# Attention and expert kernel on one core: k transposed by the DMA crossbar, one store transfer per tile, a sixth load buffer, new engine orders

## The chip, the cores and the metric

One core of a Trainium2 chip. The metric is the device time of one execution in microseconds, the median of several. Every experiment was timed in rounds beside runs of the kernel before on the same chip. A ratio is the mean time of one kernel's fast runs over the mean time of the other's fast runs in the same rounds, so it is not quite the ratio of the medians quoted beside it. The interval behind a ratio is the 95% interval. Medians are over all runs of a kernel, slow ones included.

In the profile, PE is TensorE (matrix products and transposes), PEld its weight loads, DVE is VectorE, ACT ScalarE, POOL GpSimd and SP SyncE. A `q` behind an engine's name is its instruction queue. PSUM is where the program puts the tiles that TensorE writes. The granted clock is the share of its full clock that the profile records for TensorE. A transpose by the DMA crossbar is what the traces record as DMA_TRANSPOSE.

## The reference, cut to what matters

```python
def _attn_ref(q, k, v):                      # 8 batches, 8 heads, 576 positions, 64 wide
    scores = (1 / sqrt(64)) * q @ k^T
    ret = scores * Dmat                      # Dmat = gamma[h] ** (i - j) for i >= j, else 0
    return ret @ v

def _moe_ref(x, w_in, w_out, g_ln):          # 4608 tokens, 512 -> 1024 -> 512
    h = x @ w_in
    e = exp(h - max(h)); solu = h * e / (sum(e) + 1e-9)
    ln = (solu - mean) / sqrt(var + 1e-6) * g_ln
    return ln @ w_out                        # float32 [4608, 512], 9.4 MB
```

The first result, with the heads side by side in the columns, is the x of the second part.

Of the kernel before, what the change touches and what calls it, by code (L numbers as in the profile page):

```python
# [10 lines left out]
F16 = mybir.dt.float16  # L11
P = 128
# [1 line left out]

DUR = dict(
    T=0.45, L=0.45, M1=1.73, M2=1.73, I=0.23, S=0.23, V=0.23, K=0.14, G=0.1,
    qe=1.0, xe=0.59, ex=1.22, le=1.0, oe=0.69, wi=0.6, wg=0.66, cva=0.6,
    mask=1.22, st_a=0.29, so=1.22, bn=1.68, od=0.7, wib=0.55, wgd=0.5, WM=1.73, nw=0.62, wf=0.66, wp=1.04, sqd=0.7, gc=0.2,
    sq=1.03, sk=1.03, st_b=0.4, cast=0.84, rs=0.6, cv=0.61,
    ld=0.89, ldw=1.34, out=0.72, lm=0.42,  # L20
)
PE_OUT = 0.2
PER = 5.36
START = dict(SP=2.3)
WARM = 31.0
NE = 14

FIRST = dict(
    ACT=(
        "cv0 qe0 cv1 qe1 xe0 wi1a wi2a wi0a xe1 wi3a ex0 qe2 wg0 le0 wg2 qe3 wg4 wg6 ex1 xe2 "  # L30
        "nw1 nw0 xe3 qe4 wf1 ex2 qe5 wf3 le1 xe4 qe6 wf2 ex3 le2 xe5 oe0 qe7 wf0 ex4 le3 xe6 "
        "qe8 ex5 le4 xe7 qe9 oe1 ex6 le5 oe2 qe10 xe8 ex7 le6 xe9 qe11 oe3 ex8 le7 oe4 wf6 "
        "qe12 xe10 wf4 ex9 le8 xe11 oe5 wf7 qe13 ex10 le9 xe12 wf5 qe14 oe6 ex11 le10 xe13 "
        "oe7 qe15 oe8 ex12 le11 xe14 qe16 oe9 ex13 le12 xe15 qe17 oe10 ex14 le13"
    ),
    DVE=(
        "gc sq0 sa0 sd0 sq1 mask0 wi1b sa1 sd1 mask1 wi2b wi0b wi3b sa2 sd2 so0 mask2 wg1 sa3 "
        "sd3 wg3 wg5 wg7 mask3 so1 bn0 sa4 sd4 bn1 mask4 so2 od0 sa5 sd5 mask5 bn2 sa6 sd6 "
        "so3 mask6 od1 bn3 sa7 sd7 so4 mask7 od2 bn4 sa8 sd8 so5 mask8 bn5 sa9 sd9 so6 od3 "
        "mask9 bn6 so7 od4 sa10 sd10 mask10 bn7 so8 od5 sa11 sd11 mask11 bn8 sa12 so9 sd12 "  # L40
        "od6 mask12 bn9 sa13 sd13 so10 od7 mask13 bn10 so11 sa14 sd14 od8 bn11 mask14 so12 "
        "sa15 sd15 od9 mask15 bn12 so13 od10 mask16 bn13 so14"
    ),
    PE=(
        "G K0 T0 S0 T1 I0 V0 K1 S1 I1 V1 M1_0 T2 K2 S2 L0 I2 V2 K3 T3 M1_1 S3 WM I3 V3 K4 T4 "
        "M1_2 S4 T5 M2_0 L1 I4 V4 K5 S5 T6 M1_3 I5 V5 K6 S6 L2 M2_1 T7 M1_4 I6 V6 K7 S7 L3 "
        "M2_2 T8 M1_5 I7 V7 K8 S8 L4 M2_3 T9 M1_6 I8 V8 K9 L5 S9 T10 M1_7 L6 I9 M2_4 V9 K10 "
        "S10 T11 M1_8 L7 I10 M2_5 V10 K11 S11 T12 M1_9 L8 I11 V11 K12 S12 M2_6 T13 M1_10 I12 "
        "V12 K13 S13 L9 M2_7 T14 M1_11 I13 L10 M2_8 V13 K14 S14 T15 M1_12 L11 M2_9 I14 V14 "
        "K15 S15 T16 M1_13 L12 I15 S16 V15 M2_10 T17 M1_14 L13 I16 S17 V16 M2_11"  # L50
    ),
    POOL=(
        "sk0 sk1 sm0 sc0 sm1 sc1 sq2 sk2 cv2 sk3 sm2 sc2 cv3 sq3 sm3 sc3 sk4 sq4 cv4 sq5 sk5 "
        "sm4 sc4 sq6 rs0 cv5 sk6 sq7 sm5 sc5 cv6 cv7 sk7 sm6 sk9 sc6 sk8 sq8 wp0 rs1 sm7 sc7 "
        "cv8 sq9 cv10 cv9 wp3 sm8 sk10 sc8 cv12 wp2 sq10 sq11 sq12 sm9 sc9 sk11 cv11 sk12 wp1 "
        "sm10 sc10 sk13 rs2 sq13 sq14 cv14 sm11 sc11 sk14 rs3 wp6 sm12 sc12 cv13 sq16 cv15 "
        "cv16 sm13 sc13 wp4 sk15 sq15 sk16 wp5 rs4 sm14 sc14 sq17 wp7 sk17 rs5 cv17 sm15 sc15 "
        "sq18 sk18 cv18 sq19 sk19 cv19"
    ),
    SP=(  # L60
        "ldk0 ldv0 ldq0 ldk1 ldq1 lm ldv1 lwi1 lwi2 lwi0 lwi3 ldq2 ldk2 ldv2 ldk3 lwo0 ldv3 "
        "ldq3 lwo2 lwo4 lwo6 ldk4 ldq4 ldv4 ldq5 ldk5 ldq6 ldv5 ldk6 ldv7 ldq7 ldq9 ldk7 ldk8 "
        "ldv6 ldq10 ldv8 ldk9 ldq11 ldq8 ldv10 ldk10 ldv11 ldq14 ldk11 ldk14 ldv9 ldv12 ldq12 "
        "ldk12 ldk13 ldq16 out0 out1 ldk17 ldv16 ldq15 ldq13 ldv13 out2 ldv14 ldq17 ldk16 "
        "out4 ldv15 ldk15 out3 out5 out7 out6 ldv17 ldv18 ldq19 ldk18 ldv19 ldq18 ldk19 ldq20 "
        "out8 ldk20 ldv20 out9 ldq21 ldk21 ldv21"
    ),
)
HOP = 0.06
# [104 lines left out]
def kernel(  # L174
# [10 lines left out]
    nc = tc.nc  # L185
    B, H, S, D = q.shape
    NTOK, DM = out.shape
    DFF = moe_w_in.shape[1]
    ACT = mybir.ActivationFunctionType
# [2 lines left out]
    small_np, masks_np, id_np = _np_tables()  # L192


    CAP = dict(raw=5, qk16=3, v16=4, tp=1, qkT=3, s=1, ret=2, xy=1, gw=6, s160=4, s161=9, tt=2,
               xT=5, h=1, e=2, oc=2, solu=3, sml=8, lnT=4, o=1, osb=3)
    pools = {}
    PS = bass.MemoryType.PSUM
# [13 lines left out]
    NT = 2 * NW  # L212
# [22 lines left out]
    st = [dict() for _ in range(NS)]  # L235
    tk = [dict() for _ in range(NT)]
# [43 lines left out]
    def cast_v(i, copy):  # L280
        t = pools["v16"].tile([P, 4, 2, D], F16, tag="v16", name="v16")
        copy(out=t, in_=st[i]["vr"])
        st[i]["v16"] = t

    def qk_tp(i):
        d = st[i]
        tp = pools["tp"].tile([P, 2, 2, 2, P], F16, tag="tp", name="tqk")
        for n, src in enumerate((d["q16"], d["k16"])):
            for hp in range(2):
                for j in range(2):  # L290
                    nc.tensor.transpose(  # L291
                        out=tp[:, n, hp, j], in_=src[:, j, 2 * hp : 2 * hp + 2, :], identity=ident
                    )
        d["tp"] = tp

    def qk_ev(i):
        d = st[i]
        d["qkT"] = pools["qkT"].tile([P, 2, 2, 2, P], F16, tag="qkT", name="qkT")
        nc.scalar.copy(out=d["qkT"], in_=d["tp"])  # L299


    ee = [slice(0, 64), slice(64, 128)]
# [34 lines left out]
    def scores(i):  # L337
        d = st[i]
        s_ps = pools["s"].tile([P, 2, 2, 2, P], FP, tag="s", name="s_ps")
        sv = s_ps.rearrange("p e h j (a q) -> p e h j a q", a=2)  # L340
        qkT = d["qkT"]
        for hp in range(2):
            for j in range(2):
                for c in range(2):
                    for e in range(2):
                        nc.tensor.matmul(  # L346
                            out=sv[ee[c], e, hp, j], lhsT=qkT[ee[e], 1, hp, j, ee[c]],
                            rhs=qkT[ee[e], 0, hp, :, ee[c]], start=True, stop=True,
                        )
        d["s"] = s_ps  # L350
# [171 lines left out]
    def store(t):  # L522
        w, c = divmod(t, 2)
        b, wi = wins[w]
        for j in range(2):
            q_dma = nc.scalar if t == NT - 1 and j else nc.sync
            if wi < 2:
                r0 = b * S + 256 * wi + P * c
                q_dma.dma_start(
                    out=out[r0 : r0 + P, :].rearrange("(q j) m -> j q m", j=2)[j],  # L530
                    in_=tk[t]["osb"][64 * j : 64 * j + 64],
                )
            else:
                for r in range(2):
                    r0 = (b + 2 * c + r) * S + 512
                    q_dma.dma_start(
                        out=out[r0 : r0 + 64, :].rearrange("(q j) m -> j q m", j=2)[j],
                        in_=tk[t]["osb"][64 * j + 32 * r : 64 * j + 32 * r + 32],
                    )
# [39 lines left out]
    def op(name, eng, kind, deps, key, emit, bufs=()):  # L579
        key = rank.get(name, PER * key[0] + key[1])  # L580
        ops.append(Op(name, eng, DUR[kind], [x for x in deps if x], key, emit, bufs))

    for i in range(NS):
        w, hf = divmod(i, 2)
        b, wi = wins[w]
        full = wi < 2
        op(f"ldq{i}", "SP", "ld", [], (i - 5, 0.0), lambda i=i: load(i, "q", q), [("rawq", [f"sq{i}"])])
        op(f"ldk{i}", "SP", "ld", [], (i - 5, 0.1), lambda i=i: load(i, "k", k), [("rawk", [f"sk{i}"])])
        op(f"ldv{i}", "SP", "ld", [], (i - 5, 0.2), lambda i=i: load(i, "v", v), [("rawv", [f"cv{i}"])])
        early = i < 2  # L590
        op(f"sq{i}", "DVE" if early else "POOL", "sqd" if early else "sq", [f"ldq{i}"], (i - 2, 1.8),
           lambda i=i, e=nc.vector if early else nc.gpsimd: scale(i, "q", 0, e), [("q16", [f"T{i}"])])
        op(f"sk{i}", "POOL", "sk", [f"ldk{i}"], (i - 2, 2.9), lambda i=i: scale(i, "k", 32, nc.gpsimd),
           [("k16", [f"T{i}", f"K{i}" if full else ""])])
        op(f"cv{i}", "ACT" if early else "POOL", "cva" if early else "cv", [f"ldv{i}"], (i - 1, 0.0),
           lambda i=i, c=nc.scalar.copy if early else nc.gpsimd.tensor_copy: cast_v(i, c),
           [("v16", [f"V{i}", f"K{i}" if full else ""])])
        op(f"T{i}", "PE", "T", [f"sq{i}", f"sk{i}"], (i - 1, 2.73), lambda i=i: qk_tp(i), [("tp", [f"qe{i}"])])
        op(f"qe{i}", "ACT", "qe", [f"T{i}"], (i - 1, 3.6), lambda i=i: qk_ev(i), [("qkT", [f"V{i}"])])
        op(f"S{i}", "PE", "S", [f"qe{i}"], (i, 0.3), lambda i=i: scores(i), [("s", [f"mask{i}"])])  # L600
        op(f"mask{i}", "DVE", "mask", [f"S{i}", "lm"], (i, 3.2), lambda i=i: mask(i), [("ret", [f"V{i}"])])
        if full:
            op(f"K{i}", "PE", "K", [f"sk{i}", f"cv{i}"] + [f"V{i - 1}" if i else ""], (i, 0.8), lambda i=i: kv_mm(i))
# [15 lines left out]
    for t in range(NT):  # L619
        w, c = divmod(t, 2)  # L620
        m = t + 2
# [18 lines left out]
    for c in range(4):  # L640
# [4 lines left out]
        out=masks, in_=nc.inline_tensor(masks_np, name="masks").ap().rearrange("p (m j) -> p m j", m=2)))  # L645
# [75 lines left out]
```

## The kernel before: what the change touches

The sequence is cut into 18 windows. Each has two halves of the heads, which gives 36 attention steps `i`, and two tiles of 128 tokens, which gives 36 expert tiles `t`. Sixteen windows are full, so 32 of the tiles are full. The other four tiles collect the short ends of several sequences.

Within a tile the tokens are stored even ones first: partition `64*j + q` holds row `2*q + j` of the output. This is why the store needs a pattern in `j`.

The instructions of each engine stand in an order that lists in the kernel fix (`FIRST`, cut here), with a small scheduler for the rest.

```python
def qk_tp(i):                                  # TensorE transposes q and k: eight of 128x128
    tp = pools["tp"].tile([P, 2, 2, 2, P], F16, tag="tp", name="tqk")
    for n, src in enumerate((d["q16"], d["k16"])):
        for hp in range(2):
            for j in range(2):
                nc.tensor.transpose(out=tp[:, n, hp, j],
                    in_=src[:, j, 2 * hp : 2 * hp + 2, :], identity=ident)

def qk_ev(i):                                  # ScalarE brings both out of PSUM
    nc.scalar.copy(out=d["qkT"], in_=d["tp"])

def x_ev(i):                                   # the attention result, tokens in (j, q) order
    nc.scalar.copy(out=d["xT"].rearrange("p c h q -> p c (h q)"), in_=d["av"][:, :, 0:256])

def store(t):                                  # two transfers of 64 rows for each tile
    for j in range(2):
        q_dma = nc.scalar if t == NT - 1 and j else nc.sync
        if wi < 2:
            q_dma.dma_start(
                out=out[r0 : r0 + P, :].rearrange("(q j) m -> j q m", j=2)[j],
                in_=tk[t]["osb"][64 * j : 64 * j + 64])
        else: ...                              # short tiles: four transfers of 32 rows
# ... loads: one transfer of 256 KB for each of q, k, v and full step, all issued by SyncE
```

The softmax here doesn't subtract the row's maximum and nothing guards it: scores larger than these inputs give would overflow.

## Time and profile before

| | before |
|---|---|
| median of 4 runs | 225.87 us (225.39 to 226.43) |
| span of the profiled run | 224.9 us |
| TensorE busy | 207.0 us (92%) |
| granted TensorE clock | 0.996 |
| a store, issue to landing | 2.4 us |

These lines are from the page of the kernel before. They give TensorE's and VectorE's busy time, then the busy tenths in 40 slices of 5.6 us (TensorE, granted clock, DMA), and the packets by size.

```profile
PE 207.0 (92%) x2985; PEld 121.8 (54%) x2985; DVE 181.5 (81%) x320; ACT 163.2 (73%) x238; POOL 151.8 (67%) x231
PE   7776989899699999699999999999999999999991
PEclk9999999999999999999999999999999999999998
DMA  6999999995576610799988776777763552222324
DMA packets 65635, 42.64 MB, mean 190 GB/s; under 512 B 4024, under 2 KB 59456, under 8 KB 65600
```

TensorE is nearly full from the eighteenth slice on and has no idle time at all from 106 to 205 us (busy 99.00 of 99 us). The DMA is full in the first quarter and once more, for three slices, around 105 us. Of the 4,024 packets under 512 B, 3,769 are of four bytes. The trace also records 3,761 increments of semaphores by DMA, so I take them for completion packets. In the queue q1 they are 3,696, sixteen for each of its 231 transfers. If every DMA engine that a transfer uses posts one, they count the engines of each transfer.

The next lines come from two queries of the same trace. The first is the TensorE timeline around 148 us (start, duration, line, out<-in). The second is the table of stretches (stretch, length, busy time of each engine, clock, DMA share, GB/s).

```profile
148.09 0.39 PE L291 MATMUL tqk<-ident,q_3298 128*128 128x128 f16 x4
148.31 0.39 PE L291 MATMUL tqk<-ident,k_3340 128*128 128x128 f16 x4
148.54 1.89 PE L431 MATMUL h_ps<-w_in_122,xT 128*128 128x512 f16 x8
...
153.91 1.89 PE L431 MATMUL h_ps<-w_in_122,xT 128*128 128x512 f16 x8
```

```profile
40.00:106.00 66.00, 61.20 (x952) 37.12 (x941) 62.40 (x102) 51.41 (x76) 57.72 (x82) 1.00 0.68 187
106.00:180.00 74.00, 74.00 (x1159) 45.58 (x1159) 63.53 (x114) 57.32 (x84) 56.41 (x89) 1.00 0.73 202
```

One tile follows the other at 5.37 us here. The eight transposes start at 148.09 and the next group of matmuls at 148.54, so they cost TensorE 0.45 us. Their pipelined durations overlap and must not be added up. Taking four of the eight away is worth 0.22 us a step, where TensorE alone decides. From 40 to 106 us VectorE is as full as TensorE (62.4 and 61.2 of 66 us).

The section of DMA issues of the same page shows KB for each transfer and the median time from issue to landing:

```profile
qr<-in_q_dram SPq DMA_DIRECT2D x32, 256.0 KB, 4.8
out_dram<-o_sb SPq DMA_DIRECT2D x64, 128.0 KB, 2.4
```

### The profile page before, as it was taken

To read this page: it belongs to the slowest core of one execution; us is meant where nothing else is said; L and a number is where in the kernel's file an instruction comes from. 1 tells how busy PE (TensorE), PEld (TensorE's weight loads), DVE (VectorE), ACT (ScalarE), POOL (GpSimd) and SP (SyncE) were. 2 spreads that over 40 slices of the span, in tenths; PEclk is the share of its full clock that TensorE was granted. 3 is DMA by queue.
4 is the path that set the end of the run, shared out by engine and by line. 5 is a ranking of instruction groups with operands and counts; after the bars stand their busy time and mean duration, and the time that the engine had idled before them with its cause. 6 is when DMAs were issued, how large, how long until landed. Compare 5 with 4: busy or idle time off the path is not lost.

```text
span 224.9 us, 7378 instructions
## 1 busy us (share of the span) xinstructions
PE 207.0 (92%) x2985; PEld 121.8 (54%) x2985; DVE 181.5 (81%) x320; ACT 163.2 (73%) x238; POOL 151.8 (67%) x231
## 2 busy tenths in 40 slices
PE   7776989899699999699999999999999999999991
PEld 2433445556455556465666666665666666555440
DVE  6654788999999998999999888888887888876540
ACT  3555889776869988578787777777777777776751
POOL 3429599899989989829578869695968677311010
PEclk9999999999999999999999999999999999999998
DMA  6999999995576610799988776777763552222324
GB/s 176 360 344 348 320 262 287 286 279 157 128 224 173 195 24 13 188 305 293 267 235 247 215 195 192 214 191 191 218 184 109 153 131 52 50 47 60 84 69 119
DMA packets 65635, 42.64 MB, mean 190 GB/s; under 512 B 4024, under 2 KB 59456, under 8 KB 65600
## 3 DMA queue, kind: packets, MB, share of 16 engines
q1 hardware_dynamic: 65200, 41.96, 66.9%
q8 instruction: 23, 0.38, 0.8%
q10 hardware_dynamic: 400, 0.21, 0.5%
q14 instruction: 12, 0.10, 0.2%
HBM read 32.71 MB, written 9.44 MB: 187 GB/s over the span
## 4 chain that ended last, share of the span: by engine, by line
PE 63%; DVE 17%; DMA 9%; POOL 4%; issue 2%; SPq 2%; ACT 1%; DVEq 0%; POOLq 0%; ACTq 0%
PE h_ps L431 21%; PE o_ps L501 21%; PE xy L311 6%; PE tln L480 5%; PE tqk L291 4%; DMA qr<-in_q_dram 4%; DVE solu L451 4%; PE s_ps L346 4%; DVE bs L457 3%; DVE ret L379 3%; DMA vr<-in_v_dram 3%; DMA kr<-in_k_dram 2%; DVE oc L509 2%; SPq L259 2%; DVE w L465 1%
## 5 line engine op out<-in xcount | busy, mean ns | idle before, releaser
L431 PE MATMUL h_ps<-w_in_122,xT 128*128 128x512 f16 x288 | 68.0, 379 | 2.0 <-DVE solu L451 1.9
L451 DVE TENSOR_TENSOR solu<-h_ps,e_sb 128x1024 f16<-128x1024 f32 x36 | 43.9, 1219 | 13.4 <-ACT e_sb L444 13.2
L444 ACT ACTIVATE e_sb<-h_ps 128x1024 f32<-128x1024 f32 x36 | 36.8, 1022 | 18.2 <-PE h_ps L431 17.9
L457 DVE BATCH_NORM_STATS2 bs<-solu 128x6 f32<-128x512 f16 x72 | 46.0, 680 | 0.1
L379 DVE TENSOR_TENSOR ret<-s_ps,masks 128x1024 f16<-128x1024 f32 x36 | 43.7, 1215 | 0.6 <-PE s_ps L346 0.4
L299 ACT COPY qkT<-tqk 128x1024 f16<-128x1024 f16 x36 | 36.3, 1008 | 9.3 <-PE tqk L291 9.1
L431 PEld LDWEIGHTS <-xT 128*128 128x128 f16 x288 | 27.0, 98 | 29.1 <-issue 2.8
L501 PEld LDWEIGHTS <-lnT 128*128 128x128 f16 x288 | 25.9, 98 | 27.2
L488 ACT COPY lnT<-tln 128x1024 f16<-128x1024 f16 x36 | 36.2, 1005 | 3.5 <-PE tln L480 3.5
L501 PE MATMUL o_ps<-w2c_124,lnT 128*128 128x512 f16 x160 | 38.0, 380 | 0.0
L501 PE MATMUL o_ps<-w2g_123,lnT 128*128 128x512 f16 x112 | 26.5, 380 | 0.0
L419 ACT CAST xT<-xy 128x512 f16<-128x512 f32 x36 | 21.4, 594 | 6.6 <-PE xy L311 6.2
L404 POOL TENSOR_TENSOR g<-tt,small 128x128 f32<-128x128 f32 x32 | 13.4, 418 | 15.3 <-DVE tt L400 15.3
L480 PEld LDWEIGHTS <-solu 128*128 128x128 f16 x288 | 18.5, 98 | 8.7 <-DVE solu L451 1.7
L517 ACT ACTIVATE o_sb<-o_ps,rs 128x512 f32<-128x512 f32 x20 | 13.7, 687 | 12.7 <-PE o_ps L501 6.9
L480 PE MATMUL tln<-ident,solu 128*128 128x128 f16 x288 | 22.0, 219 | 0.9 <-DVE solu L451 0.9
L346 PE MATMUL s_ps<-qkT 64*64 64x128 f16 x576 | 14.9, 220 | 0.8 <-ACT qkT L299 0.7
L346 PEld LDWEIGHTS <-qkT 64*64 64x64 f16 x576 | 9.5, 107 | 4.6 <-ACT qkT L299 1.8
L395 DVE TENSOR_TENSOR g<-xy,g 128x128 f32<-128x128 f32 x16 | 4.6, 289 | 8.7 <-PE xy L311 5.2
L400 DVE TENSOR_TENSOR tt<-xy,g 128x128 f32<-128x128 f32 x32 | 9.3, 292 | 2.7 <-ACT xT L419 0.7
L509 DVE SCALAR_TENSOR_TENSOR oc<-nws,mv,o_ps 128x512 f32<-128x512 f32 x14 | 10.3, 738 | 0.2 <-PE o_ps L501 0.2
L517 ACT ACTIVATE o_sb<-oc,rs 128x512 f32<-128x512 f32 x14 | 10.2, 728 | 0.3 <-DMA qr<-in_q_dram 0.3
(507 smaller groups left out, 336.9 us busy)
## 6 DMA issues: line engine op xcount, KB each, us to landing
kr<-in_k_dram SPq DMA_DIRECT2D x32, 256.0 KB, 4.6
vr<-in_v_dram SPq DMA_DIRECT2D x32, 256.0 KB, 4.8
qr<-in_q_dram SPq DMA_DIRECT2D x32, 256.0 KB, 4.8
out_dram<-o_sb SPq DMA_DIRECT2D x64, 128.0 KB, 2.4
w_in_f<-in_moe_w_in_dram SPq DMA_DIRECT2D x4, 512.0 KB, 5.9
w_f<-in_moe_w_out_dram SPq DMA_DIRECT2D x4, 512.0 KB, 8.0
qr<-in_q_dram SPq DMA_DIRECT2D x16, 64.0 KB, 2.3
kr<-in_k_dram SPq DMA_DIRECT2D x16, 64.0 KB, 2.0
```

The source lines that it names most:

```text
L299: nc.scalar.copy(out=d["qkT"], in_=d["tp"])
L346: nc.tensor.matmul(out=sv[ee[c], e, hp, j], lhsT=qkT[ee[e], 1, hp, j, ee[c]], rhs=qkT[ee[e], 0, hp, :, ee[c]], start=True, stop=True,)
L379: nc.vector.tensor_tensor(out=d["ret"].rearrange("p e h j q -> p (e h) (j q)"), in0=d["s"].rearrange("p e h j q -> p (e h) (j q)"), in1=ma ...
L419: nc.scalar.copy(out=d["xT"].rearrange("p c h q -> p c (h q)"), in_=d["av"][:, :, 0:256])
L431: nc.tensor.matmul(out=h_ps[:, hh], lhsT=st[2 * w + dc // 2]["xT"][:, c, dc % 2], rhs=w_in16[:, dc, hh], start=(dc == 0), stop=(dc == 3),)
L444: nc.scalar.activation(out=d["e"], in_=d["h"], func=ACT.Exp, accum_out=ws[w]["se"][:, c : c + 1])
L451: nc.vector.tensor_tensor(out=d["solu"], in0=d["h"], in1=d["e"], op=ALU.mult)
L457: nc.vector.bn_stats(out=bs[:, half], in_=tk[t]["solu"][:, half * 512 : half * 512 + 512])
L480: nc.tensor.transpose(out=tp[:, c], in_=d["solu"][:, c * P : (c + 1) * P], identity=ident)
L488: nc.scalar.copy(out=d["lnT"], in_=d["tp"])
L501: nc.tensor.matmul(out=d["o"], lhsT=d["lnT"][:, c], rhs=(w2g16 if t < NE else w2c16)[:, c], start=(c == 0), stop=(c == 7))
L517: nc.scalar.activation(out=d["osb"], in_=d["oc"] if t < NE else d["o"], func=ACT.Copy, scale=ws[t // 2]["rs"][:, t % 2 : t % 2 + 1],)
```

## The change

The intent has four parts:

1. From the seventh step on, the DMA crossbar transposes k, so that TensorE and ScalarE lose half of that work.
2. A full tile is stored by one transfer instead of two, so that the queue has fewer transfers to issue.
3. There is one more buffer for the loads.
4. The lists of engine orders are new.

```diff
-PER = 5.36
+PER = 5.14
+ND = 6
 # ... DUR: some durations for the scheduler added (cut)
 # ... FIRST: the order lists of all five engines, replaced (cut)
-    CAP = dict(raw=5, qk16=3, v16=4, tp=1, qkT=3, s=1, ...
+    CAP = dict(raw=6, qk16=3, v16=4, tp=1, qkT=3, kT=3, s=1, ...
+    def k_tp(i):
+        d["kT"] = pools["kT"].tile([P, 2, 2, P], F16, tag="kT", name="kT")
+        nc.sync.dma_start_transpose(
+            out=d["kT"].rearrange("p j h t -> p (j h) t"),
+            in_=d["k16"].rearrange("p j h d -> p (j h d)"))
     def qk_tp(i):
-        for n, src in enumerate((d["q16"], d["k16"])):
+        for n, src in enumerate((d["q16"], d["k16"]) if i < ND else (d["q16"],)):
     def qk_ev(i):
-        nc.scalar.copy(out=d["qkT"], in_=d["tp"])
+        nc.scalar.copy(out=d["qkT"][:, :n], in_=d["tp"][:, :n])      # n = 2 if i < ND else 1
     def scores(i):
+        kT = d["kT"].rearrange("p j h t -> p h j t") if i >= ND else qkT[:, 1]
     def store(t):
-        for j in range(2):
-            ...
-                q_dma.dma_start(
-                    out=out[r0 : r0 + P, :].rearrange("(q j) m -> j q m", j=2)[j],
-                    in_=tk[t]["osb"][64 * j : 64 * j + 64])
+            nc.sync.dma_start(
+                out=out[r0 : r0 + P, :].rearrange("(q j) m -> j q m", j=2), in_=tk[t]["osb"])
 # ... the operations' dependences: tk waits for sk, the scores for tk (cut)
```

In the built program the new store's output pattern has the sizes 2, 64, 512 and its input pattern 128, 1, 512. The old one had 64, 512 on both sides.

## The prediction

> **What bounds the kernel now.** The busy table gives TensorE 207.0 us of 224.9 (92%); the chain of waits is 63% TensorE. By stretches: from 106 to 205 us TensorE never rests, and one tile takes 5.3 us (h_ps matmul groups start at 132.65, 137.91, 143.16). From 40 to 100 us VectorE is as full (9.4 to 9.7 of every 10 us) and tiles take about 5.6 us. Before 34 us DMA is full. DMA is busy 0.74 to 0.78 from 120 to 160 us; no store is on the chain.
>
> **Removed.** Thirty steps lose four of eight transposes: in the timeline the eight take 0.45 us of TensorE, so 0.22 us each step, 6.7 us in all. About 18 steps lie where TensorE alone decides (4.0 us); in the VectorE-bound part perhaps 1 us counts. ScalarE's 1.0 us copy shrinks to about 0.6 (the 512-column xT copy takes 0.59), mostly off the chain. The new orders might win 1 us of idle at 86 to 95 us, where a store at the queue's head held loads back.
>
> **Added.** Thirty 128 KB crossbar transposes in the same queue. [...] No trace here shows one.
>
> **Moved, and what I think decides.** A full tile's 256 KB store becomes one transfer, whose output pattern has an outermost dimension of 2 (j), then 64 rows, against 128 partitions. [...] Before, 64 rows against 64 partitions gave 16. This trace agrees: 236 transfers left 3,769 four-byte completion packets, close to 235 x 16 + 8, the 8 being the gain vector of 8 rows.
>
> So two engines carry 64 packets of 2 KB each per store. In the packet records such a packet takes 84 to 159 ns; at 84 to 90 a store occupies both engines 5.4 to 5.8 us. The loads give each engine 96 packets of 512 B per step, at 27 ns 2.6 us. With the transpose that is about 9 us per step on two engines, against 5.3 us of TensorE. From the first store, near 43 us on: 32 stores x 5.6 = 179, remaining loads about 56, [...]together 257 us, less with overlapping packets (busy shares reach 1.09), plus gaps: an end near 290 us.
>
> **Prediction: 290 us, range 245 to 328.** Faster by over 2%: 0.13; within 2%: 0.09; slower by over 2%: 0.78. If the store still spreads over 16 engines, I expect about 220.5 us instead.
>
> **What would show it.** Right: mean DMA share well below 0.7 while stores take over 6 us from issue to landing (2.4 before) and load landings grow beyond 4.8; ScalarE's o_sb waiting for stores, POOL for loads; 2 completion packets per store instead of 32; TensorE idle from 60 us on; tiles some 8 to 9 us apart; tqk groups of four matmuls, 0.22 us. Wrong: stores landing in about 3 us, tiles 5.1 us apart from 106 us on, TensorE full.
>
> **What would make it wrong.** The split seeing the 128 partitions rather than j; two engines moving 2 KB packets far faster than 84 ns; or transposes blocking ordinary traffic (slower for another reason: transposes landing well over 3 us, all engines busy).

(What "gave 16" is the number of engines, read from the sixteen four-byte packets for each transfer.) With a time for the transposes the sum came to 257 us and to about 9 us per step on two engines. The terms that are left, stores and loads, make 235 us and 8.2 us per step.

## The result, and the profile after

| | before | after |
|---|---|---|
| median of 4 runs | 225.87 us | 316.75 us (315.34 to 320.17) |
| ratio of the fast runs | | 1.4001 (1.3939 to 1.4063) |
| TensorE busy | 207.0 us | 225.7 us |
| granted clock | 0.996 | 0.868 |
| tile to tile, middle of the run | 5.3 us | 9.2 us (22 tiles from 65.03 to 266.88 us) |

One of the four runs was slow (320.17 us) and is not in the ratio. The same lines of the page, for the changed kernel (slices of 7.9 us):

```profile
PE 225.7 (72%) x2862; PEld 124.8 (40%) x2862; DVE 177.9 (56%) x320; ACT 152.1 (48%) x238; POOL 152.1 (48%) x231
PE   8778979942960989198659949694939387899910
PEclk9999999995695899769769968796998977999975
DMA  8999898739929553755996699998973837311122
DMA packets 80993, 46.55 MB, mean 148 GB/s; under 512 B 19384, under 2 KB 74816, under 8 KB 80960
```

The kernels run much alike for the first 60 us (from 40 to 60 us TensorE is busy 18.4 of 20 us here and 18.2 before). From then on TensorE's row swings between 9 and 1 or 2. The first store is issued at 55.3 us, so the trouble begins with the stores.

TensorE does less work than before (2,862 matmuls instead of 2,985) and is still busy 18.7 us longer. The granted clock tells why: it fell where TensorE idled, and the same matmuls took longer. The clock's record in this trace falls from 1.0 to 0.5 eleven times while there is work, each time inside a gap of 2.8 us or more in TensorE's work or less than 1 us after one. A matmul of h_ps took 379 ns in the median where the record is at 1.0 and 631 ns where it is at 0.5, one of o_ps 379 and 634 ns. The two later stretches in the next lines have 0.76 and 0.81. Whether this is a consequence of the waiting and not its cause is what theory C below tests.

Stretches of the changed kernel:

```profile
40.00:60.00 20.00, 18.40 (x260) 10.60 (x259) 17.36 (x32) 16.54 (x28) 17.54 (x27) 1.00 0.99 208
80.00:100.00 20.00, 11.42 (x102) 5.60 (x100) 9.99 (x18) 5.89 (x10) 6.64 (x11) 0.76 0.73 104
100.00:140.00 40.00, 29.48 (x371) 17.01 (x372) 23.99 (x38) 17.86 (x28) 23.59 (x31) 0.81 0.54 127
```

In the stretch from 80 to 100 us no engine is busy for more than 12 of 20 us and the DMA moves 104 GB/s at a busy share of 0.73. (The kernel before had a lull in the same stretch too, 122 GB/s, but with TensorE busy 18.0 of 20 us.) Nothing is at its limit on average, so if the DMA is the limit, it must be something narrower than the average of its sixteen engines. The waits of the changed kernel (who waited for whom: total us, times, longest):

```profile
ACT o_sb L563 <- DMA out_dram<-o_sb: 29.6, 8, 6.1
POOL q_1814 L310 <- DMA qr<-in_q_dram: 11.0, 1, 11.0
PE s_ps L392 <- DMA kT<-k_1592: 10.8, 1, 10.8
POOL v_4227 L318 <- DMA vr<-in_v_dram: 7.0, 1, 7.0
```

Loads, transposes and stores are all late. ScalarE waits 29.6 us for earlier stores to give their buffers back. In the kernel before, no engine's work waited for a store. TensorE itself waits longest for transposes: the list has each buffer apart, and the query of the tile kT sums them up (total us, times):

```profile
  PE s_ps L392: 39.4, 11
```

In a_two below, with the same transposes and the old pair of stores, these waits are 5.6 us. The end of the chain of waits of the changed kernel shows the intended saving, a TensorE transpose group of four in 0.22 us, and then what it ends in:

```profile
277.94 0.22 PE tqk L335 x4
278.17 1.73 PE h_ps L477 x8
...
291.55 0.70 ACT o_sb L563
292.25 0.02 issue
292.26 14.72 DMA out_dram<-o_sb
```

By the chain, the last copy into an o_sb buffer had to wait until the store issued at 292.26 us had landed, 14.72 us later. TensorE's last matmul had ended at 300.18 us, so this wait also delays the end.

The profile's views give no engine for a packet, but the trace has the start and the duration of each. Apart from weight loads in the first 50 us, only full and short stores move packets of 2,048 bytes. I counted how many such packets were under way at once after 50 us, which takes in all 4,608 packets of the stores. The figures are us in which exactly that many were in flight:

```
in flight          1      2      3      4    5-7      8   9-11    12+
before           6.7    2.6    1.9    1.7    4.2    1.8    8.5   30.8
after            2.3  153.2   14.9    1.0    2.5    0.6    1.6    2.2
```

Before, a store's packets are in flight twelve and more at a time and are gone in a short burst. After, there are two at a time, for 153 us. The trace names no engine for a packet, so that it is the same two engines for every store is not shown directly. But had stores that were outstanding together run on different pairs, four packets at once would have been common, and they were under way for only 1.0 us. And the store issued at 292.26 us took 14.72 us to land, nearly three times the 5.4 us of its own packets (64 for each of two engines, 84 ns each).

### The profile page after: what moved, and what is told of

Its sections match the earlier page's. It is cut to its first block, busy times and chain, and to the rows that moved or that the text cites. A ratio compares the mean times of both kernels' runs of the same rounds, so it can differ in the third digit from the quotient of the medians.

```text
span 315.0 us, 7074 instructions
## 1 busy us (share of the span) xinstructions
PE 225.7 (72%) x2862; PEld 124.8 (40%) x2862; DVE 177.9 (56%) x320; ACT 152.1 (48%) x238; POOL 152.1 (48%) x231
## 2 busy tenths in 40 slices
DMA packets 80993, 46.55 MB, mean 148 GB/s; under 512 B 19384, under 2 KB 74816, under 8 KB 80960
## 3 DMA queue, kind: packets, MB, share of 16 engines
q1 hardware_dynamic: 80560, 45.89, 70.5%
## 5 line engine op out<-in xcount | busy, mean ns | idle before, releaser
L477 PE MATMUL h_ps<-w_in_125,xT 128*128 128x512 f16 x288 | 71.5, 392 | 0.6 <-DVE solu L497 0.5
L547 PE MATMUL o_ps<-w2c_127,lnT 128*128 128x512 f16 x160 | 46.6, 444 | 4.6 <-ACT o_sb L563 4.6
L547 PEld LDWEIGHTS <-lnT 128*128 128x128 f16 x288 | 29.5, 109 | 39.5 <-issue 19.1
L392 PE MATMUL s_ps<-qkT,kT 64*64 64x128 f16 x480 | 14.2, 245 | 39.4 <-DMA kT<-k_1592 10.8
L477 PEld LDWEIGHTS <-xT 128*128 128x128 f16 x288 | 28.0, 102 | 30.2 <-issue 5.8
L344 ACT COPY qkT<-tqk 128x512 f16<-128x512 f16 (+1 forms) x36 | 23.5, 653 | 23.0 <-PE tqk L335 23.0
L547 PE MATMUL o_ps<-w2g_126,lnT 128*128 128x512 f16 x112 | 30.5, 421 | 0.0
L526 PE MATMUL tln<-ident,solu 128*128 128x128 f16 x288 | 24.9, 236 | 7.7 <-ACT qkT L344 7.4
L392 PEld LDWEIGHTS <-kT 64*64 64x64 f16 x480 | 9.3, 122 | 41.1 <-DMA kT<-k_1592 10.9
L439 DVE COPY g<-xy 128x128 f32<-128x128 f32 x16 | 4.6, 290 | 35.8 <-PE xy L356 34.9
L526 PEld LDWEIGHTS <-solu 128*128 128x128 f16 x288 | 19.5, 105 | 13.3 <-issue 8.5
```

Of the source, the lines that this page charges most:

```text
L344: nc.scalar.copy(out=d["qkT"][:, :n], in_=d["tp"][:, :n])
L392: nc.tensor.matmul(out=sv[ee[c], e, hp, j], lhsT=kT[ee[e], hp, j, ee[c]], rhs=qkT[ee[e], 0, hp, :, ee[c]], start=True, stop=True,)
L477: nc.tensor.matmul(out=h_ps[:, hh], lhsT=st[2 * w + dc // 2]["xT"][:, c, dc % 2], rhs=w_in16[:, dc, hh], start=(dc == 0), stop=(dc == 3),)
L526: nc.tensor.transpose(out=tp[:, c], in_=d["solu"][:, c * P : (c + 1) * P], identity=ident)
L547: nc.tensor.matmul(out=d["o"], lhsT=d["lnT"][:, c], rhs=(w2g16 if t < NE else w2c16)[:, c], start=(c == 0), stop=(c == 7))
```

## The experiments

Four theories were to be told apart.

- **S:** the merged store runs on two DMA engines, because its output pattern's outermost size is 2. Everything else that is sent to these two engines queues behind it.
- **X:** the crossbar transposes hold up the other transfers.
- **O:** the new engine orders don't fit the chip.
- **C:** the clock fell by itself.

All the kernels below, but where it is said, give a correct result.

| kernel | transposes of k | store of a full tile | orders | median us | ratio to before |
|---|---|---|---|---|---|
| before | TensorE | two, 64 rows | old | 225.58 to 227.63 by job | 1 |
| b_one | TensorE | one, sizes 2 x 64 | old | 289.82 | 1.2746 (1.2669 to 1.2823) |
| a_two_pe | TensorE | two, 64 rows | new | 222.24 | 0.9781 (0.9732 to 0.9829) |
| a_two_pe_raw5 | TensorE | two, 64 rows, five buffers | new | 222.51 | 0.9853 (0.9778 to 0.9928) |
| a_one_pe | TensorE | one, 2 x 64 | new | 284.91 | 1.2567 (1.2492 to 1.2643) |
| a_j4_pe | TensorE | one, 4 x 32 | new | 239.08 | 1.0549 (1.0451 to 1.0648) |
| a_j16_pe | TensorE | one, 16 x 8 | new | 222.22 | 0.9817 (0.9760 to 0.9875) |
| a_two | crossbar | two, 64 rows | new | 232.07 | 1.0235 (1.0166 to 1.0304) |
| after | crossbar | one, 2 x 64 | new | 316.75 | 1.4001 (1.3939 to 1.4063) |
| a_j4 | crossbar | one, 4 x 32 | new | 266.12 | 1.1706 (1.1616 to 1.1795) |
| a_j8 | crossbar | one, 8 x 16 | new | 233.89 | 1.0350 (1.0268 to 1.0431) |
| a_j16 | crossbar | one, 16 x 8 | new | 222.10 | 0.9761 (0.9700 to 0.9822) |
| a_nat | crossbar | one, 128 rows | new | 221.15 | 0.9763 (0.9685 to 0.9841) |
| a_nat_act | crossbar | one, 128 rows, by ScalarE's queue | new | 242.04 | 1.0597 (1.0505 to 1.0689) |

The medians of after, a_j16, a_j4 and a_nat contain one slow run each. Two of the four runs of a_nat_act were slow; its fast ones took 239.20 and 239.94 us. Kernels from different jobs ran on different chips, where the kernel before differed by up to 2 us: b_one, a_two, a_two_pe and a_j16 are one job; a_one_pe, a_j16_pe, a_j4 and a_j8 another; the remaining four experiments a third.

### b_one: the kernel before with the merged store alone

```diff
-        for j in range(2):
-            ... dma_start(out=out[r0 : r0 + P, :].rearrange("(q j) m -> j q m", j=2)[j],
-                          in_=tk[t]["osb"][64 * j : 64 * j + 64])
+            nc.sync.dma_start(
+                out=out[r0 : r0 + P, :].rearrange("(q j) m -> j q m", j=2), in_=tk[t]["osb"])
```

> The kernel before with only the merged store. Theory S: 32 stores of 5.6 us and 2.6 us of loads per step on two engines, without the transposes' share[...]: about 290 us (270 to 310); 4-byte packets 3,769 - 64 x 16 + 32 x 2 = 2,809. Rivals X, O: within 2% of before, about 225 us.

It took 289.82 us, ratio 1.2746. The merged store alone costs 62 us against the 227.63 us of before in the same rounds, without any transpose and with the old orders. That is about two thirds of the 91 us by which the changed kernel is slower. From the page of b_one, with ScalarE's wait for stores from its list of waits:

```profile
DMA  7999999435331137444444457745342311111122
DMA packets 64674, 42.63 MB, mean 148 GB/s; under 512 B 3064, under 2 KB 58496, under 8 KB 64640
q1 hardware_dynamic: 64240, 41.95, 47.8%
ACT o_sb L517 <- DMA out_dram<-o_sb: 51.6, 17, 6.2
```

This is the first half of the proof by counting. The packets under 512 B fell from 4,024 to 3,064, by 960. If each of 64 transfers posted 16 completions before, and each of 32 posts 2 now, the difference is 64 x 16 - 32 x 2 = 960. The trace's four-byte packets are 2,809. The DMA row, mostly 1 to 5 tenths from the eighth slice on, fits: most engines idle while two are the limit. The average share of the queue is 47.8% for a kernel that the DMA limits.

### a_two: the changed kernel with the old pair of stores

```diff
-            nc.sync.dma_start(
-                out=out[r0 : r0 + P, :].rearrange("(q j) m -> j q m", j=2), in_=tk[t]["osb"])
+            for j in range(2):
+                nc.sync.dma_start(
+                    out=out[r0 : r0 + P, :].rearrange("(q j) m -> j q m", j=2)[j],
+                    in_=tk[t]["osb"][64 * j : 64 * j + 64])
```

> The changed kernel with the full tile's store put back to two transfers of 64 rows[...]; all else of the change is kept. Theory S (the merged store runs on two DMA engines): the time falls from 317 to about 221 us (217 to 226), store landing back to 2 to 3 us, granted clock back above 0.98, 4-byte packets about 30 x 32 + 2745 + 1024 = 4,729. Rival X (the crossbar transposes hold the other transfers up) and rival O (the new engine orders do not fit the chip): it stays near 300 us or above, with kT still waited for some 10 us at a time. Rival C (the clock fell by itself): the clock stays near 0.87 and the time above 250 us.

It took 232.07 us, with the clock back at 0.990 and 4,729 four-byte packets, as expected. Theories X (as the whole cause), O and C are out: 85 of the 91 us are gone with the store alone. But I had expected 217 to 226, and it is slower than the kernel before by 2.35% (1.7 to 3.0%, so whether by over 2% stays unclear). There is something more, and it appears only together with the crossbar, as the next kernel shows.

### a_two_pe and a_two_pe_raw5: the orders, and the buffer

```diff
 # a_two, and
-ND = 6
+ND = 36          # no step uses the crossbar
 # a_two_pe_raw5 also:
-    CAP = dict(raw=6, ...
+    CAP = dict(raw=5, ...
```

> The changed kernel with two transfers per store and with all transposes on TensorE again, so that only the new orders and the sixth load buffer are left of the change. Theory S: within 2% of before, about 224 us (221 to 228), tiles 5.3 us apart from 106 us on. Rival X: also about 224 us, while a_two stays slow. Rival O: well above 240 us.

> a_two_pe (222.2) with five load buffers instead of six: only the new engine orders are left of the change. If the orders alone give the gain over before: 222 to 223.5. If the sixth buffer is needed for it: 224.5 or more.

They took 222.24 and 222.51 us. The new orders are good: they give 1.5 to 2.2% over the kernel before (a gain is certain, over 2% is not), and within these intervals the sixth buffer adds nothing. The gain lies in the stretch before 106 us, where TensorE used to wait. From a_two_pe's table of stretches:

```profile
40.00:106.00 66.00, 65.11 (x996) 39.37 (x997) 62.50 (x104) 55.34 (x82) 60.76 (x86) 1.00 0.78 205
106.00:180.00 74.00, 73.69 (x1112) 44.25 (x1109) 66.03 (x114) 58.61 (x85) 57.39 (x91) 1.00 0.70 193
```

TensorE is busy 65.1 of 66 us from 40 to 106 us, against 61.2 before. These 3.9 us are nearly all of the 4.3 us by which the spans of the two profiled runs differ.

The two kernels also show what a transpose by the crossbar leaves. Under 512 B a_two has 20,344 packets and a_two_pe 4,024. The 16,320 more are 15,360 of 256 B and 960 of four bytes, so 512 and 32 for each of the thirty transposes.

### a_j16, a_j8, a_j4: the same single transfer with another outermost size

```diff
-                out=out[r0 : r0 + P, :].rearrange("(q j) m -> j q m", j=2), in_=tk[t]["osb"]
+                out=out[r0 : r0 + P, :].rearrange("(q j) m -> j q m", j=16), in_=tk[t]["osb"]
 # a_j8: j=8; a_j4: j=4. The rows land in a permuted order: wrong on purpose.
```

One number changes. Bytes, rows, size of the transfer and number of dimensions stay. A rival to S, that a large or three-dimensional store is slow in itself, is tested by this.

> The changed kernel, its single store transfer kept, but with the rows of the output split in 16 groups instead of 2: the same bytes and rows of 2 KB, outermost size 16[...]. The rows land permuted, so the result is wrong on purpose. Theory S: about 220 us (216 to 226), as fast as a_two or up to 1 us faster; 4-byte packets about 30 x 32 + 2745 + 512 = 4,217. Rival M (one transfer of 256 KB with a pattern of three dimensions is slow whatever its engines): about 300 us while a_two is fast. Rivals X, O: about 300 us or more.

> The same with 8 groups[...] (rows permuted, wrong on purpose). Theory S: store 1.35 us, with loads and transpose 4.7 us per step, under TensorE's 5.3: 221 to 226 us, next to a_j16's 222.1. 4-byte packets 2745 + 960 + 32 x 8 = 3,961.

> The changed kernel with its single store transfer split in 4 groups of rows instead of 2 (rows permuted, wrong on purpose)[...]. Theory S, by the same sum as the prediction, per step and engine: store 32 packets x 0.084 = 2.7 us, loads 2.6, [...]so 6.1 us against 5.3 of TensorE; [...]so about 215 plus the gaps that made 317 of 290: 225 to 245 us. 4-byte packets 2745 + 960 + 32 x 4 = 3,833. A rival in which only the value 2 is special, or the pattern's form is to blame: 222 or 317.

The time for the transposes is in the 6.1 us of a_j4 and the 4.7 us of a_j8 per step; with it the sum of a_j4 came to 164 us from 43 us on. That 16, 8 and 4 groups mean as many engines was an assumption, which the counts below test.

The times are 222.10, 233.89 and 266.12 us for 16, 8 and 4, against 316.75 for 2. The rival is out: the same single transfer of 256 KB is harmless with 16. The packets of 2,048 bytes in flight, counted as above, in us:

```
in flight          1      2      3      4    5-7      8   9-11    12+
b_one           14.5  149.0   14.8    0.9    1.6    0.5    1.3    2.1
after   (j=2)    2.3  153.2   14.9    1.0    2.5    0.6    1.6    2.2
a_j4    (j=4)    3.5   19.0   12.9   76.6   12.4    0.3    1.4    3.2
a_j8    (j=8)    6.3    3.2    2.0    3.6   19.7   32.0    8.8    3.7
a_j16  (j=16)    8.1    2.6    2.7    2.2    5.0    2.2    5.2   25.0
```

The most frequent number is 2, 4, 8, and for 16 the group of 12 and more. The completion packets agree. The next lines are from the pages of a_j4, a_j8 and a_j16, in that order:

```profile
DMA packets 81058, 46.55 MB, mean 178 GB/s; under 512 B 19449, under 2 KB 74881, under 8 KB 81025
```

```profile
DMA packets 81185, 46.55 MB, mean 202 GB/s; under 512 B 19576, under 2 KB 75008, under 8 KB 81152
```

```profile
DMA packets 81441, 46.55 MB, mean 212 GB/s; under 512 B 19832, under 2 KB 75264, under 8 KB 81408
```

Over the changed kernel's 19,384 these are 65, 192 and 448 more. 32 stores with 2, 6 and 14 more engines each, one packet for each engine, make 64, 192 and 448.

Two of the three expectations missed: a_j4 by 21 us over the upper end of its range, a_j8 by 8. That of a_j16 held for the time, but not in that it would be at most 1 us faster than a_two: it is 10.0 us faster. My sum adds the mean load of an engine and says that there is no loss until an engine has more work for a step than TensorE. That is too kind, as the following kernels show.

### a_one_pe, a_j4_pe, a_j16_pe: the same stores without the crossbar

```diff
 # the changed kernel (j=2), a_j4 and a_j16, each with
-ND = 6
+ND = 36
```

> The changed kernel with all transposes on TensorE: the merged store on two engines, the new orders and the sixth buffer. Theory S with the crossbar as an additional load on the same two engines: near b_one's 290 us (280 to 298), so that the transposes are worth 20 to 35 us of the changed kernel's 317. If the new orders are what separates b_one from the changed kernel, it stays at 310 to 320.

> a_j4 (266.1 us) with all transposes on TensorE; rows permuted, wrong on purpose. Theory I[...]: without it only the sum of those four engines counts, 2.7 us of store and 2.6 us of loads per step, about TensorE's 5.3 us: 222 to 235 us. Theory A (costs add on the engines as in the prediction's sum[...]): 240 to 250. If the transposes have no part in it: 260 or more.

> All transposes on TensorE, new orders, sixth buffer, and one store transfer over 16 engines (rows permuted, wrong on purpose). Theory Q (the queue's own time matters only where the crossbar transposes fill it, so the shorter store buys nothing here): 221.5 to 222.5, like a_two_pe. If the single transfer helps by itself: below 220.5. In either case the crossbar gains nothing over it where a_j16 (222.1) is not faster.

They took 284.91, 239.08 and 222.22 us. The last two also have permuted rows. The crossbar's own cost is the difference to the same store with it: 31.8 us for two engines (316.75 - 284.91), 27.0 us for four (266.12 - 239.08), and nothing for sixteen (222.10 and 222.22). The two kernels of each pair ran in different jobs; worked out from their ratios to the kernel before instead (times 226 us), it is 32, 26 and -1 us.

For a_j4_pe theory I (that the transposes turn the uneven load of the four engines into waits) expected 222 to 235 us. Theory A (that the costs add up on these engines) expected 240 to 250. The result lies between them, nearer to A, but neither is shown. Even without the crossbar, four engines that hold 5.3 us of work per step (an estimate: 32 packets of 84 ns and 96 of 27 ns) against TensorE's 5.3 us cost 17 us (239.08 against 222.22). Why they do is not shown.

What the crossbar costs where it limits nothing can be read in a_two and a_j16. Its transposes in a_two, from the query of the tile kT (issue on the queue, minimum, median and maximum in ns; then landing in us):

```profile
L324 SPq DMA_TRANSPOSE kT<-k x30: 1195/1220/3674, 34.6 to 194.5; - x30
DMA to landing us min/median/max: 2.4/3.1/7.4
```

A transpose holds the issuing queue for 1.2 us; a store's issue takes 0.55. So a full tile of a_two asks the one queue for about three loads of 0.5 to 0.6 us, one transpose of 1.2 and two stores of 0.55. That is 3.8 to 4.1 us of 5.3 before any wait, a sum from the durations in the timeline. The queue's timeline in a_two around 124 us:

```profile
122.92 0.59 SPq L295 DMA_DIRECT2D vr<-in_v_dram  x1
123.56 1.17 SPq L295 DMA_DIRECT2D kr<-in_k_dram  x2
124.83 1.22 SPq L324 DMA_TRANSPOSE kT<-k  x1
126.15 1.17 SPq L574 DMA_DIRECT2D out_dram<-o_sb  x2
127.38 0.58 SPq L295 DMA_DIRECT2D qr<-in_q_dram  x1
128.06 2.14 SPq L324 DMA_TRANSPOSE kT<-k  x1
130.31 1.18 SPq L574 DMA_DIRECT2D out_dram<-o_sb  x2
131.57 1.94 SPq L582 DMA_DIRECT2D out_dram<-o_sb  x4
```

There are no gaps of more than 0.13 us. The durations of the issuing instructions, added up from 106 to 200 us, fill 90% of that time in a_two, 81% in a_j16 and 59% in a_two_pe. The second part of the change, fewer transfers, has a use where the crossbar is in use. With the crossbar, one store instead of two is worth 10.0 us (232.07 to 222.10). Without it, it is worth nothing (222.24 and 222.22). That the two act together is shown by these four runs. That it is the queue's time is the reading that I prefer, from the timeline; it is not isolated, for a pair of stores also takes two completion semaphores where one store takes one (in the traces of before and after each transfer posts to one of eight, in turn).

### a_nat: the intent with the fault mended

The tokens are put in the order of the output's rows when the attention result leaves PSUM. Partition and row then agree, and the store is one transfer with 128 rows outermost on both sides.

```diff
     def x_ev(i):
-        nc.scalar.copy(out=d["xT"].rearrange("p c h q -> p c (h q)"), in_=d["av"][:, :, 0:256])
+        for c in range(2):
+            nc.scalar.copy(
+                out=d["xT"][:, c].rearrange("p h (q j) -> p h j q", j=2),
+                in_=d["av"][:, c, 0:256].rearrange("p (h j q) -> p h j q", h=2, j=2))
     def store(t):
-                out=out[r0 : r0 + P, :].rearrange("(q j) m -> j q m", j=2), in_=tk[t]["osb"])
+            nc.sync.dma_start(out=out[r0 : r0 + P, :], in_=tk[t]["osb"])
 # short tiles: two transfers of 64 rows instead of four of 32
```

> The changed kernel with its intent kept and its fault mended, correct result: the xT copy writes the tokens in the order of the output's rows (two copies of 256 columns with a step of two elements instead of one of 512), so the single store has 128 rows outermost on both sides[...]; the short tiles store two transfers of 64 rows. Theory S: like a_j16 (222.1), plus at most 2 us for the extra copies on ScalarE: 221.5 to 224.5.

It took 221.15 us with a correct result, 0.35 us below the expected range, ratio 0.9763. The interval of the ratio (0.9685 to 0.9841) reaches over 0.98, so "faster by over 2%" is not certain; that it is faster is. It beats both kernels. It can't be told from a_two_pe, which has no crossbar at all (222.24, ratio 0.9781, another chip). So the crossbar as such has brought nothing that these runs can show. The trace of a_nat tells where TensorE's saved 0.22 us a step went:

```profile
106.00:180.00 74.00, 72.68 (x1108) 42.33 (x1107) 66.06 (x115) 55.95 (x102) 57.31 (x92) 1.00 1.07 227
```

The matmuls of this stretch are fewer, but TensorE now idles 1.3 of 74 us where the kernel before has no idle time. The DMA share is 1.07, where before it was 0.73. The share is the sum of the packets' durations as a share of sixteen engines' time. At 1.07 the packets overlap, so it is not a measure of work alone. The transposes account for the rise in GB/s from 202 to 227: fifteen of them fall into this stretch, 7,680 packets of 256 B, which are 27 GB/s. It may be that the DMA has taken the place of TensorE as the thing that holds the pace. This is argued from one line and not shown by a run, and TensorE is still busy for 98% of the stretch.

### a_nat_act: the stores on another queue

```diff
 # a_nat, and
-            nc.sync.dma_start(out=out[r0 : r0 + P, :], in_=tk[t]["osb"])
+            nc.scalar.dma_start(out=out[r0 : r0 + P, :], in_=tk[t]["osb"])
```

> a_nat with the full tiles' stores issued by ScalarE's queue, right behind the copy that they wait for, instead of the queue that issues loads and transposes. Theory Q (what the crossbar's saving of 0.22 us a step on TensorE loses is lost to the time of the one issuing queue, 1.2 us for each transpose): faster than a_nat, 217 to 221. If the queue's time no longer matters once the store is single: the same as a_nat within 1 us, or slower by ScalarE's 0.6 us per store.

It took 242.04 us: a clear miss, in the wrong direction. Waits of the load queue in a_nat_act:

```profile
SPq L579 <- ACT o_sb L565: 29.8, 2, 29.5
SPq L324 <- POOL sbd L459: 16.7, 6, 8.0
SPq L324 <- POOL k L310: 13.9, 4, 8.3
```

The queue of loads and transposes is held longer than before at its heads. One store of a short tile stood there for 29.5 us by the profile, and transposes stood up to 8.3 us. In the built program a transfer also waits for the completion semaphore that an earlier transfer, now often of the other queue, has in use (in the trace of before 226 of the queue's 231 transfers wait for the one of the eight to which they will post), and the engine orders were made for the other placement. Which of the two it is was not separated. This is left open. Theory Q is neither confirmed nor refuted by it.

## Why the prediction was right

**The mechanism held.** Forecast 290 us, 245 to 328, 78% for slower; measured 316.75. The step on which all hung was that the merged store runs on two engines. It was the author's assumption, with one small sign in the trace of before, the 3,769 four-byte packets. The runs confirm it by three kinds of evidence: the count of completions (960 four-byte packets fewer in b_one), the packets in flight (2, 4, 8 and 12 or more for outermost sizes 2, 4, 8 and 16), and the times (316.75, 266.12, 233.89, 222.10).

**The stated alternative held too.** "If the store still spreads over 16 engines, about 220.5 us": a_j16 has 222.10 and a_nat 221.15. It came to nearly the right number by luck, though. I had put 5 us on the saved transposes and 1 us on the orders. In fact the orders alone give about 2% (222.24), and the crossbar adds nothing that can be measured.

**The size was 27 us too small.** The terms of the sum, one by one:

- The start was misread. The sum begins at "the first store, near 43 us". At 43.3 us the trace of before has the first copy into an o_sb buffer; its first store is issued at 54.7 us. In the changed kernel it is 55.3 us, in b_one 54.2 and in a_one_pe 47.8. This makes the sum up to 12 us too small.
- The stores were put slightly too high. A 2 KB packet takes 84 ns in the median in these three kernels, so 32 stores of 64 packets are 172 us and not 179. The loads that follow the first store are 57 to 61 us (their packets at 27 ns), against 56.
- The discount was wrong. With the start, stores and loads as measured, b_one comes to 283 us and a_one_pe to 281, against spans of 288.9 and 283.1. So there are gaps of 2 to 6 us and no net gain from overlapping packets, for which I had taken off some 10 us.
- The transposes: their term was an assumption that no trace on hand showed. Measured: 31.8 us (after against a_one_pe), 1.06 us each. This is the term of the mechanism that was mis-sized, 10 us too small. Each transpose leaves 512 packets of 256 B, 18 ns long by their median. Spread evenly over sixteen engines, which is an estimate, that is 32 for each and 0.58 us. But in the changed kernel such a packet takes 41 ns in the mean, against 26 ns in a_j16. I read the rest as waiting. The cost of a transpose depends on how uneven the load of the engines is: 31.8 us with two engines, 27.0 with four, none with sixteen.

**The signs in the profile:**

- Right: ScalarE's o_sb waits for stores (29.6 us); POOL waits for loads (11.0 us once); TensorE has gaps of several us from 67 us on; tiles are 9.2 us apart (forecast 8 to 9); transpose groups of four take 0.22 us.
- Right by way of counting: 2 completion packets for a store instead of 32 for the pair.
- Wrong: the DMA share. I said well below 0.7; the changed kernel's queue shows 70.5%. In b_one, without transposes, it is 47.8%. The packets of the transposes last 41 ns in the mean where the median is 18, and the share counts all of it as busy.
- Not to be read: the times from issue to landing of stores and loads, for which the profile of after gives none. The 14.72 us of one store at the end of the chain stand in for them.

**Where the expected gain went:** with the fault mended, TensorE's busy time is indeed less (201.1 us in a_nat against 206.1 in a_two_pe), and the time is the same within what the runs resolve. What holds the pace in its place was not shown.

## What to carry to other kernels

Look at the outermost size of both access patterns of every DMA before merging transfers. One transfer of 256 KB whose output pattern begins with 2 ran on two engines (2 four-byte packets for each store) and cost this kernel 62 us (b_one), while the two transfers that it replaced ran on sixteen each (16 four-byte packets). If a merge needs a small outer dimension, change the layout earlier, in a copy that is made anyway, so that 128 rows come first (a_nat: 221.15 us against 316.75). When average shares say that nothing is full and yet all transfers are late, count packets in flight and completion packets, for an average over sixteen engines hides two that are at their limit (47.8% in b_one, with two packets of the stores in flight for 149.0 us).
